# Moving the six hash-bit transfers of each head pair from SyncE's DMA queue to GpSimd's, in a hash attention with a PReLU feed-forward

## The chip, the cores and the metric

The kernel runs on one core of a Trainium2 chip. The metric is the device time of one execution in microseconds (us), as the median of several runs. Five engines work side by side: PE (TensorE) multiplies matrices, DVE (VectorE) and ACT (ScalarE) work on elements, POOL (GpSimd) does odd jobs, and SP (SyncE) only issues DMAs. A DMA can be issued from SP, ACT or POOL. Each engine takes its instructions in order, and an instruction that has to wait holds up everything behind it on the same engine. That is true of SP's queue of DMA issues as well.

## The reference

For 4 batches, 8 heads, 768 positions and 64 dimensions, queries attend only to keys with the same hash bucket of six bits. The result is put through a feed-forward layer with a PReLU.

```python
q_bits = (np.einsum('bhsd,dk->bhsk', q, proj) > 0)       # proj: 64 x 6
k_bits = (np.einsum('bhsd,dk->bhsk', k, proj) > 0)
q_bucket = np.sum(q_bits * 2 ** np.arange(6), axis=-1)   # k_bucket likewise
mask = q_bucket[:, :, :, None] == k_bucket[:, :, None, :]
scores = np.where(mask, np.matmul(q, k^T) / 8, -1e9)
attn = softmax(scores)                                   # sum + 1e-9
x = (attn @ v), heads side by side                       # 3072 x 512
h = x @ w_in                                             # 512 x 2048
out = (np.maximum(h, 0) + alpha * np.minimum(h, 0)) @ w_out
```

## The kernel before

The program computes a guarded fast path, `fast_path`; a second path, `general_path`, would run only if a flag computed on the way said that the inputs are out of the range of the fast one. The profiled execution is the fast path.

It has two stages. In the first, which takes up to about 343 us, it goes through 16 pairs of heads (`pi`), and between them prepares the weights. In the second it runs the two products of the feed-forward layer, on PE nearly without a gap. Most compute instructions are kept in the order in which the program text has them, by a helper called `do`. DMAs are not written through `do` in the place of the change; the scheduler puts each into its queue.

The mask is not applied as such. Each query and each key gets a vector of plus and minus ones from its hash bits, and one extra bf16 matmul adds their product to the scores; where the bits agree the exponent is kept, elsewhere it falls far below. So `scores` needs, for every pair, the hash bits in the layout of its own matmuls: `qb`, one of two buffers of 128 x 768 bf16 whose other rows stay zero, and `kb`, a single buffer of 128 x 1152 bf16. In `kb` the columns are three parts of 384: part 0 and part 1 hold the key bits of the two halves of the positions, and part 2 is where the second half arrives from the Sign.

For pair `pi + 1` this is done while pair `pi` is being attended. In order on PE for one pair:

1. `scores` (L742): 12 cells, a cell being a key block `kc` (0 to 5) and a query half `g` (0 or 1), in the order kc 0 g 0, kc 0 g 1, kc 1 g 0 and so on. In a cell each of two heads has a bf16 matmul of the bits (`sc<-qb,kb`) and an fp32 matmul (`sc<-qT,kT`). ACT takes the exponent (L745).
2. `hash_bits` of the next pair (L704): 16 matmuls in the profile. ACT turns the result into signs (L710) and writes parts 0 and 2 of `kb`. Then six DMAs put the bits into place: four `qb<-kb` of 24 KB (L715) and two `kb<-kb` of 48 KB (L717).
3. `turn` of the pair after that: transposes of q and k (L674).
4. `attend` of this pair (L775): 96 matmuls, about 7.9 us.
5. `totals` (L789): row sums of the exponents, after DVE has added them up (L757, L758, L761, L764).

Then the scores of the next pair follow. The first cell reads query bits of half 0 (the first two DMAs, one for each head), the second cell those of half 1 (the third and the fifth), and the cells from kc 3 on read key bits of half 1 (the fourth and the sixth).

Before the change all six stand in SP's queue, beside these others: the loads of q and k (L499) and v (L488), loads of raw weights (`load_weight`, L566), stores of prepared weights (L634 and L647) and stores of the attention output (L823). In most pairs the built order on SP is three L715, one L566, then L717, L715, L717; in four pairs an L634 stands behind that L566. The weight work that these wait for is on DVE: `weight_clamp` (L590), `weight_parts` (L596), `weight_sum` (L621 and L624).

For the first pair, the bits are written by ACT and DVE directly (L723, L729) and no such DMA is issued. The other 15 pairs use the six DMAs each: 60 of L715 and 30 of L717 in all.

POOL has only some memsets at the start and, in the second stage, 16 DMAs of 512 KB: `load_out` (L962) and `sum_out` (L969).

Of the kernel before, what the change touches and what calls it, by code (L numbers as in the profile page):

```python
# [407 lines left out]
def fast_path(  # L408
# [12 lines left out]
    nc = tc.nc  # L421
    P = 128
    B, H, S, D = q.shape
# [56 lines left out]
    nat, tr, bits = {}, {}, {}  # L480
# [58 lines left out]
    raw, wx, wr = {}, {}, {}  # L539
# [122 lines left out]
    def two_banks(name):  # L662
        return psum.tile([P, 2, 512], F32, name=name, tag="sc", bufs=3)
# [23 lines left out]
    def hash_bits(pi, halves=BOTH, engine=None):  # L687

        if halves.start == 0:
            bits["q", pi] = qbs[pi % 2]
            kb = pool.tile([P, 3 * CW], BF16, name=f"kb{pi}", tag="kb", bufs=1)
            bits["k", pi] = kb[:, :S]
            bits["raw", pi] = kb.rearrange("p (a w) -> p a w", w=CW)
        ps = {"k": two_banks(f"hs{pi}")}
        ps["q"] = psum_av.tile([P, 2, 512], F32, name=f"hsq{pi}", tag="av") if engine is DVE else ps["k"]
        for half in range(halves.start, halves.stop):
            for name in "qk" if engine is DVE else "kq":
                for s in range(2):  # L700
                    r, c = D * s, D * (s ^ half) + 32 * "kq".index(name)

                    for t, c in [("k", c)] + ([("q", c ^ D)] if engine is DVE and name == "q" else []):
                        do(PE.matmul(  # L704
                            ps[t][c : c + 32, half if t == "k" or engine is not DVE else 0, :CW], wh[r : r + D],
                            tr[name, pi][r : r + D, half * CW : (half + 1) * CW], start=True, stop=True,
                        ))
        if engine is None:
            raw = bits["raw", pi]
            do(ACT.activation(raw[:, 0:3:2], ps["k"][:, :, :CW], AF.Sign, bias=hb))  # L710
            for half in range(2):
                for s in range(2):
                    c = D * (s ^ half)
                    cols = slice(half * CW, (half + 1) * CW)
                    nc.sync.dma_start(bits["q", pi][D * s : D * s + 32, cols], raw[c + 32 : c + 64, 2 * half])  # L715
                    if half:
                        nc.sync.dma_start(bits["k", pi][D * s : D * s + D, cols], raw[c : c + D, 2])  # L717
            return
        for half in range(halves.start, halves.stop):
            cols = slice(half * CW, (half + 1) * CW)  # L720
            for s in range(2):
                c = D * (s ^ half ^ (engine is DVE)) + 32
                do(ACT.activation(  # L723
                    bits["q", pi][D * s : D * s + 32, cols], ps["q"][c : c + 32, 0 if engine is DVE else half, :CW], AF.Sign, bias=hb[c : c + 32],
                ))

            for to, c, n in [(0, 0, P)] if half == 0 else [(0, D, D), (D, 0, D)]:
                dst, src = bits["k", pi][to : to + n, cols], ps["k"][c : c + n, half, :CW]
                do(DVE.tensor_scalar(  # L729
                    dst, src, hb_k[c : c + n, 0:1], hb_k[c : c + n, 1:2], op0=ALU.is_gt, op1=ALU.subtract,  # L730
                ))
# [383 lines left out]
    for half in (first, second):  # L1115
        turn(0, "q", half)
        turn(0, "k", half, DVE)
        if half is first:
            nil[0]()
            hash_bits(0, first, DVE)  # L1120
# [10 lines left out]
    ahead = [(kc, 0) for kc in range(CH)]  # L1131
    scores(0, ahead)
    hash_bits(0, second, DVE)
    turn(1, "q")
    turn(1, "k", BOTH, DVE)
# [4 lines left out]
    for pi in range(NPAIR):  # L1140
# [26 lines left out]
        if pi + 1 < NPAIR:  # L1167
            hash_bits(pi + 1)
# [126 lines left out]
```

## Time and profile before

| What | Value |
|---|---|
| time, median of 3 runs | 897.59 us (897.15 to 897.98) |
| time of the profiled execution | 897.64 us |
| its span, first to last instruction | 895.8 us |
| PE busy | 884.2 us, 99% |
| DVE busy | 746.8 us, 83% |
| ACT busy | 379.5 us, 42% |
| POOL busy | 14.4 us, 2% |
| mean granted clock of PE | 0.997 |
| L715, `qb<-kb` on SP | 60, median 585 ns each to issue, 2.4 us to landing |
| L717, `kb<-kb` on SP | 30, median 560 ns each to issue, 3.5 us to landing |

The span is what the profile shows from the first instruction to the last; the time of the same execution is 1.84 us longer. In lines of the timeline and the chain of waits the first number is the start in us from the beginning of the span and the second is the duration in us; `x3` is a number of merged instructions. `SPq` is an issue on SP's queue. In lists of waits the three numbers are the total in us, how often, and the longest. In the views of one source line, a duration is given as the least, the median and the largest, in ns. An issue ends when the issuing engine is done with it; the data lands later, and "to landing" counts from the start of the issue.

### The profile page before, as it was taken

The numbers are of one execution on the slowest core, as the hardware profiler recorded it, in microseconds if no ns is written. First come the engines' busy times: TensorE is split into PE (matmuls) and PEld (weight loads), VectorE is DVE, ScalarE is ACT, GpSimd is POOL, SyncE is SP. The second block draws the span as 40 slices with busy tenths as digits, with TensorE's granted clock in tenths as the row PEclk, the third lists the DMA queues.
The fourth block names the chain that finished last, engine by engine and source line by source line (L and its number), as shares of the span: only waits on it lengthen the run. The fifth ranks groups of instructions, "written<-read, shape, count | busy, mean of one in ns | idle before, by whom it ended". The sixth has DMA issues, their size and how long they took to land.

```text
span 895.8 us, 15331 instructions
## 1 busy us (share of the span) xinstructions
PE 884.2 (99%) x5886; PEld 598.5 (67%) x5886; DVE 746.8 (83%) x1266; ACT 379.5 (42%) x668; POOL 14.4 (2%) x30
## 2 busy tenths in 40 slices
PE   9999999999999999999999999999999999999996
PEld 4544545555555545557997557997557998556996
DVE  5888888888989887899989678988668989768996
ACT  7877777788877762222112222112222111222111
POOL 1000000000000001120000000000000000000000
PEclk9999999999999999999999999999999999999998
DMA  8444575575685625587333435343525242430242
GB/s 235 139 143 129 151 232 153 149 229 173 204 281 163 202 74 185 181 296 289 141 113 107 163 111 166 107 147 88 178 88 192 95 159 80 157 116 0 95 143 72
DMA packets 126177, 137.22 MB, mean 153 GB/s; under 512 B 78976, under 2 KB 110224, under 8 KB 122512
## 3 DMA queue, kind: packets, MB, share of 16 engines
q1 hardware_dynamic: 121376, 126.59, 44.9%
q0 software_dynamic: 2304, 8.39, 2.6%
q10 hardware_dynamic: 2416, 1.18, 0.5%
q8 instruction: 48, 0.79, 0.3%
q14 instruction: 33, 0.27, 0.1%
HBM read 104.87 MB, written 28.31 MB: 149 GB/s over the span
## 4 chain that ended last, share of the span: by engine, by line
PE 84%; DVE 9%; issue 3%; ACT 2%; DMA 2%; SPq 0%; DVEq 0%; ACTq 0%
PE sc L742 12%; PE av L775 10%; PE f_0a L875 2%; PE z_4a L875 2%; PE z_7a L875 2%; PE z_3a L875 2%; PE z_6a L875 2%; PE z_5a L875 2%; PE f_4a L875 2%; PE f_3a L875 2%; PE f_2a L875 2%; PE f_1a L875 2%; PE z_2a L875 2%; PE f_5a L875 2%; DMA qb<-kb 2%
## 5 line engine op out<-in xcount | busy, mean ns | idle before, releaser
L745 ACT ACTIVATE pt<-sc 128x768 f32<-128x768 f32 x192 | 154.8, 812 | 53.5 <-PE sc L742 53.2
L742 PE MATMUL sc<-qT,kT 64*128 64x384 f32 x768 | 155.8, 483 | 0.0
L775 PE MATMUL av<-pt,vn 128*32 128x385 f32 (+1 forms) x1536 | 127.4, 486 | 0.0
L742 PEld LDWEIGHTS sc<-qT,kT 64*128 64x128 f32 x768 | 70.0, 187 | 40.9 <-issue 40.7
L775 PEld LDWEIGHTS av<-pt,vn 128*32 128x32 f32 x1536 | 48.7, 109 | 71.1 <-issue 70.5
L928 DVE TENSOR_TENSOR g<-g,g 128x384 f32<-128x384 f32 x128 | 68.4, 555 | 2.2
L742 PE MATMUL sc<-qb,kb 64*128 64x384 bf16 x384 | 66.5, 323 | 2.4 <-DMA qb<-kb 2.1
L992 DVE TENSOR_TENSOR gs<-g,gs 128x768 f32<-128x768 f32 x56 | 53.3, 952 | 1.0
L992 DVE TENSOR_TENSOR gs<-g 128x768 f32<-128x768 f32 x56 | 53.3, 951 | 0.0
L984 DVE TENSOR_TENSOR ws<-wl 128x512 f32<-128x512 f32 x56 | 38.5, 687 | 17.5 <-DMA wl<-w_out_s 15.9
L753 DVE TENSOR_TENSOR accp<-pt,pt 128x1536 f32<-128x1536 f32 x16 | 28.1, 1759 | 17.5 <-ACT pt L745 17.5
L924 DVE SCALAR_TENSOR_TENSOR g<-h,alpha 128x384 f32<-128x384 f32 x32 | 19.7, 616 | 25.1 <-ACT h L917 25.1
L742 PEld LDWEIGHTS <-kb 64*128 64x128 bf16 x384 | 20.9, 94 | 25.9 <-issue 4.3
L580 ACT ACTIVATE wr<-raw 128x512 int32<-128x512 uint32 x32 | 22.8, 712 | 17.2 <-issue 16.0
L758 DVE TENSOR_TENSOR accd<-accd,pt 128x1536 f32<-128x1536 f32 x16 | 28.1, 1759 | 2.0 <-ACT wr L580 0.5
L761 DVE TENSOR_TENSOR accp<-accp,pt 128x1536 f32<-128x1536 f32 x16 | 28.0, 1753 | 0.0
L757 DVE TENSOR_TENSOR accd<-pt,pt 128x1536 f32<-128x1536 f32 x16 | 28.0, 1752 | 0.0
L764 DVE TENSOR_TENSOR accd<-accd,accp 128x1536 f32<-128x1536 f32 x16 | 28.0, 1751 | 0.0
L805 DVE STREAM_TRANSPOSE st<-sm 128x192 f32<-128x192 f32 x32 | 10.3, 361 | 16.9 <-PE sm L789 16.9
L875 PE MATMUL f_0a<-x,wi 128*128 128x384 f32 x64 | 23.5, 489 | 0.0
L875 PE MATMUL f_4a<-x,wi 128*128 128x384 f32 x64 | 23.3, 486 | 0.0
L875 PE MATMUL f_1a<-x,wi 128*128 128x384 f32 x64 | 23.3, 486 | 0.0
(348 smaller groups left out, 1732.1 us busy)
## 6 DMA issues: line engine op xcount, KB each, us to landing
wi<-w_in_s SPq DMA_DIRECT2D x32, 896.0 KB, 4.7
wl<-w_out_s SPq DMA_DIRECT2D x16, 1024.0 KB, 4.8
wl<-w_out_r SPq DMA_DIRECT2D x12, 1024.0 KB, 4.9
raw<-in_moe_w_out_dram SPq DMA_DIRECT2D x16, 512.0 KB, 3.9
raw<-in_moe_w_in_dram SPq DMA_DIRECT2D x16, 512.0 KB, 4.0
w_in_s<-wsi SPq DMA_DIRECT2D x16, 448.0 KB, 5.8
vn<-in_v_dram SPq DMA_DIRECT2D x16, 384.0 KB, 4.2
x_s<-x SPq DMA_DIRECT2D x16, 384.0 KB, 2.8
```

The source lines that it names most:

```text
L742: do(PE.matmul(sc[:, s, :CW], what["k", pi][r, ks], what["q", pi][r, qs], start=first, stop=not first,))
L745: do(ACT.activation(pts[kc][:, g, :, :CW], sc[:, :, :CW], AF.Exp, scale=SCALE / DOWN))
L753: do(DVE.tensor_tensor(accp[pi], p(0), p(1), op=ALU.add))
L757: do(DVE.tensor_tensor(accd[pi], p(3), p(4), op=ALU.add))
L758: do(DVE.tensor_tensor(accd[pi], accd[pi], p(5), op=ALU.add))
L761: do(DVE.tensor_tensor(accp[pi], accp[pi], p(2), op=ALU.add))
L764: do(DVE.tensor_tensor(accd[pi], accd[pi], accp[pi], op=ALU.add))
L775: do(PE.matmul(av[pi][D * s + t : D * s + t + 32, g, :w], nat["v", pi][:, s, kc * D + t : kc * D + t + 32], pts[kc][:, g, s, :w], start=(k ...
L875: do(PE.matmul(self.ps[bank], self.left(left, k), self.right(right, k), start=start and k == 0, stop=k == self.nk - 1, skip_group_check=no ...
L928: do(DVE.tensor_tensor(new_g(b, to)[:, i], g_m[b, x][:, i], g_m[b, y][:, i], op=ALU.subtract))
L984: do(DVE.tensor_tensor(t, w2[b, n, x], w2[b, n, y], op=op))
L992: do(DVE.tensor_tensor(t, g2[b, n, x], g2[b, n, y], op=ALU.subtract))
```

## The change

In `hash_bits`, the six DMAs of a pair are issued with `nc.gpsimd.dma_start` in place of `nc.sync.dma_start`. What they copy, and what they must wait for, is as before.

```diff
                 for s in range(2):
                     c = D * (s ^ half)
                     cols = slice(half * CW, (half + 1) * CW)
-                    nc.sync.dma_start(bits["q", pi][D * s : D * s + 32, cols], raw[c + 32 : c + 64, 2 * half])
+                    nc.gpsimd.dma_start(bits["q", pi][D * s : D * s + 32, cols], raw[c + 32 : c + 64, 2 * half])
                     if half:
-                        nc.sync.dma_start(bits["k", pi][D * s : D * s + D, cols], raw[c : c + D, 2])
+                        nc.gpsimd.dma_start(bits["k", pi][D * s : D * s + D, cols], raw[c : c + D, 2])
             return
```

## The prediction

> **What bounds the kernel now.** I read the page first, for the engine that never rests and for the chain that ended last.
>
> ```profile
> PE 884.2 (99%) x5886; PEld 598.5 (67%) x5886; DVE 746.8 (83%) x1266; ACT 379.5 (42%) x668; POOL 14.4 (2%) x30
> ...
> PE 84%; DVE 9%; issue 3%; ACT 2%; DMA 2%; SPq 0%; DVEq 0%; ACTq 0%
> ```
>
> PE is busy for 884 of 895.8 us, so only what makes PE wait, or what it stops waiting for, can move the end. POOL does almost nothing. Next, who PE waited for: of all DMAs, only those the change moves.
>
> ```profile
> PE sc L742 <- DMA qb<-kb: 2.1, 4, 1.1
> ```
>
> So four of the 15 pairs that hash their bits through DMA start their scores late. The chain of waits, cut to one of them, shows how:
>
> ```profile
> 89.67 0.70 DVE wso L624
> ...
> 90.39 0.38 SPq L634
> ...
> 90.87 0.51 SPq L717
> ...
> 91.43 4.09 DMA qb<-kb
> ...
> 95.56 0.59 PE sc L742 x2
> ```
>
> SP's queue holds, in this order: three bit copies (numbers 1 to 3), the weight load L566, in the four late pairs also the weight store L634, then copies 4 to 6 (L717, L715, L717). L566 waits for DVE's L621 and L634 for DVE's L624, so copies 4 to 6 stand behind DVE work that has nothing to do with them. SP's own timeline in a pair where PE is not late has the same hole:
>
> ```profile
> 64.53 2.42 SPq L715 DMA_DIRECT2D qb<-kb  x3
> ...
> 69.07 0.33 SPq L566 DMA_DIRECT2D raw<-in_moe_w_in_dram  x1
> 69.50 0.51 SPq L717 DMA_DIRECT2D kb<-kb  x1
> 70.05 0.59 SPq L715 DMA_DIRECT2D qb<-kb  x1
> 71.10 0.50 SPq L717 DMA_DIRECT2D kb<-kb  x1
> ```
>
> The Sign (L710) ends at 64.51. Copy 5 is issued 5.5 us later although its data was there at once; it lands 3.3 us on, at 8.8. PE needs copies 1 and 2 at 73.39 (8.9 us after the Sign, the first cell of scores), 3 and 5 at 74.20 (9.7, the second cell, query half 1), 4 and 6 only at the seventh cell, 4.0 us further (13.7). In the pair at 85.11 the L634 store pushes copy 5 to 91.43 and its landing to 4.1 us: it lands at 95.52, 10.4 after the Sign, past 9.7.
>
> What the lateness costs is seen in the period. The chain has the attend steps at these starts:
>
> ```profile
> 64.91 7.89 PE av L775 x96
> ...
> 106.87 7.89 PE av L775 x96
> ...
> 127.48 7.89 PE av L775 x96
> ```
>
> An undisturbed pair takes 20.61 us (106.87 to 127.48). The two pairs from 64.91 to 106.87 take 41.96, 0.75 more than two undisturbed ones. By the same sums the chain gives 0.66 (127.48 to 169.35) and 0.61 (231.17 to 272.99). In the fourth, PE's timeline has attend at 293.53 and 314.05: 20.52, in a pair without the 1.46 us of transposes, so 1.37 late. **Together 3.4 us.** The 2.1 in the list of waits is less because the rest shows as longer matmuls around the wait.
>
> **What the Trainium skill says.** "DMA: Bandwidth & Descriptors", section "Issuing engines are not separate DMA queues": DMAs from any engine run on the same 16 DMA engines; another issuer saves only sequencer time. The trace agrees that issue order is what hurts here. The same page, "Queues, rings and completion order", has each queue's ring consumed in order and the DMA engines taking turns between rings. That fits copy 5 landing in 4.1 us behind the 512 KB L566 and L634, against a 1.8 us minimum for L715; no run here shows the turns themselves. Its section "Anatomy of one DMA — SWDGE (gpsimd) path" prices a GpSimd DMA at about 2.0 us plus bytes over 436 GB/s. For 512 KB that is an estimate of 3.2; the fastest of L962 took 3.7. "SBUF — State Buffer", section "Who interferes with whom": a VectorE operation in a two-port mode and a GpSimd instruction exclude each other from a shared port pair, and descriptor writing is such an instruction; operations with two SBUF inputs conflict only with GpSimd reads. In the trace DVE's two-input sums keep their length beside POOL's DMAs (L928: 2.21 us for four, at 362.98 beside one and at 353.64 beside none); no one-input case stands beside a POOL DMA.
>
> **The change part by part.** The built program keeps the order of all instructions on PE, DVE and ACT. 60 copies of L715 and 30 of L717 leave SP and stand on POOL between its memsets and L962.
>
> *Removed from SP:* 90 issues at about 0.58 us, some 52 us of queue time. This is worth nothing by itself: no engine waits for SP's other loads in this stage. They go some 2 us earlier in each pair (qn at 69.4 instead of 71.7), and the weight load L566 still waits for DVE. vn is first read by attend two pairs, some 40 us, later.
>
> *Added to POOL:* six issues per pair. The nearest rows are those of the other GpSimd DMAs:
>
> ```profile
> L962 POOL DMA_DIRECT2D wo<-w_out_r x8: 751/756/890, 348.1 to 392.6; - x8
> ...
> DMA to landing us min/median/max: 3.7/6.8/10.8
> ```
>
> and POOL's timeline, in which they follow each other without a gap:
>
> ```profile
> 348.07 3.13 POOL L962 DMA_DIRECT2D wo<-w_out_r  x4 [345.23 <-DVE x L822]
> ```
>
> So 0.78 us per issue, for 512 KB; 24 and 48 KB have fewer rows and should not cost more. POOL has nothing else until L962 at 348, after the last copy (321), so nothing useful queues behind. The waits on POOL are the Sign for copy 1, PE's previous scores for copy 4 (over before the Sign) and semaphores of older copies, some 0.04 us each, 0.2 in all. Starts after the Sign: 0, 0.8, 1.6, 2.5, 3.3, 4.1. From start to landing: below, the page's price, 2.0 + 0.06; above, the fastest 512 KB row, 3.7. Copy 5 lands at 5.4 to 7.0, and I take 6.4. It is needed at 9.7, so 2.7 to 4.3 us are spare. Copy 2 lands at 2.9 to 4.5 against 8.9, copy 6 at 6.2 to 7.8 against 13.7. The cover is the 7.9 us of attend and the row sums on PE.
>
> *Removed from PE:* the four late starts, **-3.4 us**. Eleven pairs with the same engine work show 20.6 us without a wait, so nothing else is late next at that place; the rest of the kernel is PE's and moves up.
>
> *DVE beside POOL's descriptors:* the only one-input SBUF operation on DVE in POOL's 4.9 us is L596, which at 0.42 us for 512 elements runs faster than the 0.69 of L621.
>
> ```profile
> 67.89 0.42 DVE L596 TENSOR_SCALAR wx<-wx 128x512 uint32<-128x512 uint32 x1
> ...
> 69.68 1.75 DVE L764 TENSOR_TENSOR accd<-accd,accp 128x1536 f32<-128x1536 f32 x1
> ```
>
> It starts 3.4 us after the Sign, amid copy 5's issue. If it must wait for one issue, it is up to 0.8 late. L764 ends at 71.43 and the row sums start at 72.62, so 1.2 us are spare. The exception is the last hashed pair, where the waits name L764 once (0.2 us): 0.1 spare there, up to 0.7 lost once. I take 0; bounds 0 and +0.7.
>
> Sum: -3.4, bounds -3.8 (better landings of other loads) and -2.7. Against the profiled execution, 897.64 (span 895.8 and 1.84 outside), that is 894.2; the median of the runs, 897.59, is the same within 0.05.
>
> **Rivals.**
> *Slower: GpSimd's transfers are serial.* If its 2.0 us are paid one after another, copy 5 lands at 5 x 2.06 = 10.3, 0.6 past need, in all 15 pairs: +9.0 - 3.4, 903.2. It decides from a landing at 9.9 (15 x 0.23 = 3.4). Against it: the four L962 issues in 3.13 us. For it: no small GpSimd transfer is in the trace.
> *No change: L596 is held for almost two issues.* At 1.35 us the row sums come 0.16 late in 14 pairs and 1.2 in the last: 3.4, 897.6. A hold of 1.5 would give 899.9. Against it: POOL is done 1.5 us after L596's start, and the port should change hands between two issues.
> *Part of the gain:* in the four late pairs another thing (the L634 store with L566, now issued close to the q and k loads) delays PE by half: 895.9.
> That the transfers do not move is excluded by the built order.
>
> **How the numbers follow.** Full gain 0.70 (893.5 to 895.0); part 0.08; held DVE 0.10; serial transfers 0.12. About 0.2%, 1.8 us, is what a measurement can tell from no change: faster is below 895.8, slower above 899.4. Faster 0.70 + 0.03; within 0.05 + 0.07 + 0.01; slower 0.11 + 0.03. The likeliest is 894.2. The range from 893.4 to 897.6 takes in the full and the partial gain and half of the held DVE, some 0.82.
>
> **What would show it.** Right: PE's wait for the copies gone, attend every 20.6 us in all pairs, POOL busy for some 70 us more at about 0.78 us an issue, copy 5 landing 5 to 7 us after L710, L596 within 1 us of its place. Wrong: PE waiting for qb or kb in most pairs, landings over 9 us, issues over 1.5 us, or a new wait of the row sums for L764.

## The result, and the profile after

| | before | after |
|---|---|---|
| median of 6 runs | 897.79 us (897.15 to 899.33) | 894.12 us (893.48 to 894.80) |
| ratio after / before, 95% interval | | 0.9959 [0.9948, 0.9971] |
| profiled execution, its span | 897.64, 895.8 us | 893.73, 891.9 us |
| first Sign to last Sign (ends of L710 on ACT) | 23.50 to 315.18, 291.68 us | 23.03 to 311.33, 288.30 us |

The change makes the kernel 3.7 us faster (2.6 to 4.7 by the interval); 894.2 was predicted. The profiled executions differ by 3.9 in their spans. Of this, 291.68 - 288.30 = 3.4 lies between the first and the last Sign, where the change works. Another 0.47 lies ahead of the first Sign, where the change moves nothing. It is not a part of the gain: in the repeat of the changed kernel below, the first Sign ends at 23.37, and the stretch between the Signs is 288.28 again. This part goes with the clock. The trace's record of the granted clock begins, with the full clock, at 7.22 us in the profile before and at 6.29 in the one after, and the L704 matmuls at about 6.1 us take 0.85 us before and 0.57 after. Half of the 0.93 between these two times is the 0.47; in seven of the twelve profiles of this case the first Sign ends 19.9 us plus half of that time into the span.

The page of the kernel after, engines and chain by engine:

```profile
PE 882.5 (99%) x5886; PEld 594.7 (67%) x5886; DVE 746.8 (84%) x1266; ACT 379.8 (43%) x668; POOL 59.6 (7%) x120
...
PE 93%; DVE 5%; issue 1%; ACT 1%; ACTq 0%; DVEq 0%
```

DMA and SPq, 2% and 0% of the chain before, no longer stand in it. POOL has 90 instructions more and 59.6 - 14.4 = 45.2 us more busy time. The list of PE's waits (total in us, how often, the longest):

```profile
PE nil L515 <- DVE hb L519: 1.2, 1, 1.2
PE z_2c L875 <- DVE m L1013: 0.5, 1, 0.5
PE sm L789 <- DVE accd L764: 0.2, 1, 0.2
PE sc L742 <- DVE kb L729: 0.2, 1, 0.2
```

The wait for `qb<-kb` is gone and none has come in its place. In the chain of waits no attend step comes late any more; between the second and the third of these stand the scores that were late before:

```profile
64.45 7.89 PE av L775 x96
...
85.06 7.89 PE av L775 x96
...
105.66 7.89 PE av L775 x96
```

Twice 20.6, and so in all pairs with the same work on PE; only the second step (20.8, with one more matmul, L535) and the last two (19.15 and 18.8, with fewer) differ. POOL's timeline in that pair, whose Sign ends at 84.65 (in brackets: how long POOL had been idle, and what ended it):

```profile
84.94 1.48 POOL L715 DMA_DIRECT2D qb<-kb  x3 [17.49 <-ACT kb L710]
86.53 0.52 POOL L717 DMA_DIRECT2D kb<-kb  x1
87.05 0.50 POOL L715 DMA_DIRECT2D qb<-kb  x1
87.54 0.52 POOL L717 DMA_DIRECT2D kb<-kb  x1
```

And SP's timeline after the same Sign:

```profile
89.24 0.33 SPq L566 DMA_DIRECT2D raw<-in_moe_w_out_dram  x1
89.93 0.38 SPq L634 DMA_DIRECT2D w_out_r<-wso  x1
90.40 2.04 SPq L499 DMA_DIRECT2D qn<-in_q_dram  x2
```

All six copies are issued by 88.06, 3.4 us after the Sign, and so ahead of L566 and L634, which wait for DVE as before. What one issue costs, and how long after its start the data lands, from the view of line L715:

```profile
L715 POOL DMA_DIRECT2D qb<-kb x60: 496/501/658, 23.7 to 313.7; - x60
...
DMA to landing us min/median/max: 1.6/1.9/4.2
```

Half a microsecond an issue, and 1.9 us in the middle to landing, where SP's copies of the same line needed 2.4. Copy 5 lands 4.0 to 4.4 us after the Sign in nine pairs and 5.2 to 6.0 in six; PE needs it at 9.7.

### The profile page after: what moved, and what is told of

Its sections match the earlier page's. It is cut to its first block, busy times and chain, and to the rows that moved or that the text cites. A ratio compares the mean times of both kernels' runs of the same rounds, so it can differ in the third digit from the quotient of the medians.

```text
span 891.9 us, 15377 instructions
## 1 busy us (share of the span) xinstructions
PE 882.5 (99%) x5886; PEld 594.7 (67%) x5886; DVE 746.8 (84%) x1266; ACT 379.8 (43%) x668; POOL 59.6 (7%) x120
## 4 chain that ended last, share of the span: by engine, by line
PE 93%; DVE 5%; issue 1%; ACT 1%; ACTq 0%; DVEq 0%
PE sc L742 17%; PE av L775 13%; PE f_0a L875 2%; PE z_4a L875 2%; PE z_7a L875 2%; PE z_3a L875 2%; PE z_6a L875 2%; PE z_5a L875 2%; PE f_4a L875 2%; PE f_3a L875 2%; PE f_2a L875 2%; PE f_1a L875 2%; PE z_2a L875 2%; PE f_5a L875 2%; PE z_1a L875 2%; PE f_7a L875 2%
## 5 line engine op out<-in xcount | busy, mean ns | idle before, releaser
L742 PEld LDWEIGHTS sc<-qT,kT 64*128 64x128 f32 x768 | 68.1, 187 | 39.5 <-issue 39.4
L742 PE MATMUL sc<-qb,kb 64*128 64x384 bf16 x384 | 63.3, 323 | 0.3 <-DVE kb L729 0.2
L715 POOL DMA_DIRECT2D qb<-kb x60 | 29.8, 502 | 264.6 <-ACT kb L710 264.6
L742 PEld LDWEIGHTS <-kb 64*128 64x128 bf16 x384 | 19.0, 94 | 27.8 <-issue 4.3
L764 DVE TENSOR_TENSOR accd<-accd,accp 128x1536 f32<-128x1536 f32 x16 | 28.0, 1751 | 0.0
L805 DVE STREAM_TRANSPOSE st<-sm 128x192 f32<-128x192 f32 x32 | 10.3, 361 | 17.2 <-PE sm L789 17.2
```

What stands on the lines that cost most here:

```text
L715: nc.gpsimd.dma_start(bits["q", pi][D * s : D * s + 32, cols], raw[c + 32 : c + 64, 2 * half])
L742: do(PE.matmul(sc[:, s, :CW], what["k", pi][r, ks], what["q", pi][r, qs], start=first, stop=not first,))
```

## The experiments

The question after the result was not whether PE's wait had gone, but why: is it GpSimd's ring, or the place of the copies ahead of other transfers? And is the margin of 4 to 6 us that is now seen a margin that can be used?

### Four ways to take copy 5 out from behind the store

**Only the store moved.** The six copies stay on SP; the weight stores L634, eight in all, go to GpSimd. One of them stood ahead of copies 4 to 6 in each of the four late pairs.

```diff
-                nc.sync.dma_start(w_out_r[:, :, n].rearrange("m p d -> p m d"), wst[HW + n])
+                nc.gpsimd.dma_start(w_out_r[:, :, n].rearrange("m p d -> p m d"), wst[HW + n])   # L634
```

> The kernel before, with only the eight stores L634 issued by GpSimd; all six bit copies stay on SyncE, still behind L566. Theory (copies 4 to 6 are late only where the store stands ahead of them in SP's queue): copy 5 lands 8.8 us after the Sign in all pairs, under the 9.7 at which it is needed, PE's four late starts vanish, -3.4 us, ratio to before 0.9962. Rival (GpSimd's path is what makes the copies arrive earlier, or SP's 52 us of relieved issue time is what counts): the four late pairs stay, ratio 1.000.

Measured: 893.95 us, ratio 0.9956 [0.9942, 0.9970] (before in these runs: 897.75). SP's timeline in the pair whose store is at 89.59 on POOL:

```profile
84.03 1.86 SPq L715 DMA_DIRECT2D qb<-kb  x3
88.58 0.33 SPq L566 DMA_DIRECT2D raw<-in_moe_w_out_dram  x1
89.01 0.50 SPq L717 DMA_DIRECT2D kb<-kb  x1
89.56 0.58 SPq L715 DMA_DIRECT2D qb<-kb  x1
```

L566 still stands ahead of copies 4 to 6, and copy 5 still lands 8.4 to 9.2 us after the Sign in all pairs but the first and the last, but that is before 9.7, and PE does not wait for a copy. So the 3.4 us are the price of L634's place in the queue, and copies that land late but in time cost nothing.

**Only copy 5 moved.**

```diff
-                    nc.sync.dma_start(bits["q", pi][D * s : D * s + 32, cols], raw[c + 32 : c + 64, 2 * half])
+                    (nc.gpsimd if half and s else nc.sync).dma_start(bits["q", pi][D * s : D * s + 32, cols], raw[c + 32 : c + 64, 2 * half])
```

> The kernel before, with only copy 5 of each pair (L715, second half, second head; 15 DMAs) issued by GpSimd. Theory (the second cell's wait for copy 5 is the whole cost; copies 4 and 6 have 13.7 us): -3.4 us, ratio 0.9962, copies 4 and 6 still landing 10 to 11 us after the Sign in the four pairs with the store, without anyone waiting. Rival (copies 4 and 6 matter too, or all six must leave SP): less than half of the gain, ratio over 0.998.

Measured: 894.13 us, ratio 0.9959 [0.9946, 0.9973]. Copies 4 and 6 still land 10.0 to 11.1 us after the Sign in the four pairs, and nobody waits for them: they are read at 13.7. One transfer of the six carries the whole gain.

**All six on SP, ahead of the bulk.** The weight load and the store are written after `hash_bits`, and GpSimd is not used.

```diff
-        load_weight(i + 4)
         ...
         if pi + 1 < NPAIR:
             hash_bits(pi + 1)
+        load_weight(i + 4)
+        while later:                     # the L634 stores, kept in a list
+            nc.sync.dma_start(*later.pop(0))     # L1170
```

> The kernel before, all six copies on SyncE, but the weight load L566 and the store L634 put behind the six in SP's queue; orders on PE, DVE, ACT and POOL unchanged. Theory (it is the place in the queue, not the issuing engine): copy 5 issued about 2.5 to 3 us after the Sign, landing at 5, no wait of PE for the copies, ratio 0.9962, the same as the change within 0.0015. The weight load goes some 0.5 us later at most, since it waits for DVE until 4.5 us after the Sign and the six issues end at about 3.8. Rival (GpSimd's own ring, or freed SP time, is needed): copies land behind other transfers, gain under half.

Measured: 893.39 us, ratio 0.9951 [0.9937, 0.9964]. SP's timeline:

```profile
84.53 1.85 SPq L715 DMA_DIRECT2D qb<-kb  x3
86.48 0.55 SPq L717 DMA_DIRECT2D kb<-kb  x1
87.08 0.59 SPq L715 DMA_DIRECT2D qb<-kb  x1
87.71 0.59 SPq L717 DMA_DIRECT2D kb<-kb  x1
89.06 0.33 SPq L566 DMA_DIRECT2D raw<-in_moe_w_out_dram  x1
89.79 0.38 SPq L1170 DMA_DIRECT2D w_out_r<-wso  x1
```

The hole of the profile before lies behind the copies now. Copy 5 lands 4.3 to 5.8 us after the Sign, where GpSimd had 4.0 to 6.0. The time cannot be told from that of the change.

**The change once more**, in the same runs, as their measure.

> The changed kernel once more, beside the three above on one chip. All theories: 0.9959 as before within its interval, about 894.1 us. The profiled execution before and after also differ by 0.46 us ahead of the first hashed pair (matmuls of 0.85 us against 0.57 at about 6 us): if that is chance, the time from the first to the last L704 step is the same in this profile as in the first one while the start moves.

Measured: 893.90 us, ratio 0.9958 [0.9944, 0.9972]. The four intervals all lie on each other. What issues the copies is not the reason of the gain; that they, or copy 5 alone, no longer stand behind L634 is.

### Only the harmless copies moved

The opposite test: copies 1 to 3, which never were late, on GpSimd, and 4 to 6 left on SP.

```diff
-                    nc.sync.dma_start(bits["q", pi][D * s : D * s + 32, cols], raw[c + 32 : c + 64, 2 * half])
+                    (nc.sync if half and s else nc.gpsimd).dma_start(bits["q", pi][D * s : D * s + 32, cols], raw[c + 32 : c + 64, 2 * half])
```

> The kernel before, with copies 1, 2 and 3 of each pair on GpSimd and copies 4, 5 and 6 left on SyncE. Theory: copies 1 to 3 were never late (they land 1.8 to 5.7 us after the Sign, needed at 8.9 and 9.7), so nothing is gained: ratio 1.000, PE still waits for qb in four pairs. Rival (relieving SP of 26 us of issue, or GpSimd's ring, brings the gain): about half of -3.4, ratio 0.998.

Measured: 894.23 us, ratio 0.9965 [0.9953, 0.9977] (before: 897.49), the full gain. The expectation missed, and SP's timeline says why:

```profile
84.89 0.51 SPq L717 DMA_DIRECT2D kb<-kb  x1
85.46 0.59 SPq L715 DMA_DIRECT2D qb<-kb  x1
86.09 0.59 SPq L717 DMA_DIRECT2D kb<-kb  x1
89.42 0.34 SPq L566 DMA_DIRECT2D raw<-in_moe_w_out_dram  x1
```

With three issues fewer on SP, the scheduler put copies 4 to 6 ahead of L566, not behind it. The kernel that was run was not the one that was meant. So it was built once more, with the store, the weight load and copies 4 to 6 held in the order of the program text:

```diff
-            nc.sync.dma_start(raw[i], piece(i))
+            do(nc.sync.dma_start(raw[i], piece(i)))                # L566; L634 and copies 4 to 6 likewise
```

> Copies 1 to 3 on GpSimd, copies 4 to 6 on SyncE, as in the earlier run of that name, in which the built order had also moved copies 4 to 6 ahead of L566. Here their place behind L566 and L634 is fixed by program order. Theory (only the place of copies 4 to 6 in SP's queue costs): copy 5 is issued about 5.5 us after the Sign, 6.3 in the four pairs with the store, PE waits there as before, ratio 1.000 (0.998 to 1.001). Rival (taking copies 1 to 3 off SP is worth something by itself, as the earlier run seemed to say): ratio 0.9965.

Measured: 899.79 us, ratio 1.0027 [1.0019, 1.0035] (before: 897.23). No gain but a small loss, outside the expected 0.998 to 1.001 on the side away from the rival. SP's timeline in a pair with a store, and PE's waits for the copies:

```profile
89.90 0.38 SPq L634 DMA_DIRECT2D w_out_r<-wso  x1
90.37 0.46 SPq L566 DMA_DIRECT2D raw<-in_moe_w_out_dram  x1
91.01 0.56 SPq L717 DMA_DIRECT2D kb<-kb  x1
91.62 0.59 SPq L715 DMA_DIRECT2D qb<-kb  x1
```

```profile
PE sc L742 <- DMA qb<-kb: 4.0, 3, 2.3
```

Here copies 4 to 6 are behind both bulk transfers, copy 5 is issued 7.0 us after the Sign (84.61) where it was 6.3 before, and PE is late. That holds in three pairs, which lose 0.97, 1.23 and 4.27 us. Together 6.5 against 3.4 before: the loss comes from the pinned order, which puts L634 ahead of L566 and the copies later still. The order was not held everywhere: in four of the 15 pairs the built program has copies 4 to 6 right after the Sign, ahead of both. One of these is among the four that were late before (Sign at 251.75, L634 at 257.10). Its copy 5 is issued 0.6 us after the Sign, and PE does not wait:

```profile
252.34 0.59 SPq L715 DMA_DIRECT2D qb<-kb  x1
```

So within one kernel, with copies 1 to 3 on GpSimd in every pair, PE is late where copy 5 stands behind L634 and L566 and on time where it does not. Moving three copies to GpSimd with the others left behind L634 gains nothing.

In the pair that loses 4.27 us, only 2.6 are lost at the second cell. The rest is lost by the seventh, where the granted clock is 0.50 for 3.4 us (306.6 to 310.0) after PE's wait of 2.3.

### Is the margin real? GpSimd's copies made later

The prediction called 2.7 to 4.3 us spare, and the profile after shows more. To use up some of it, POOL waits for the Sign with a small copy and then writes zeros to a new tile that nobody reads, 0.74 us each, before it issues the six copies; these go through `do`, so that they stay behind.

```diff
+            do(POOL.tensor_copy(idle[0:32, 0:1], raw[0:32, 2, 0:1]))
+            for _ in range(2):                                       # 4 and 10 in the other two
+                do(POOL.memset(idle, 0.0))
```

The lines move by up to 5: the copies are L720 and L722, the scores L747, L596 is L598, L764 is L769.

> The changed kernel, with one small copy that waits for the Sign and two memsets of 0.73 us ahead of the six transfers on GpSimd (the results of this idle work are not used). The six issues then run from about 2.0 to 5.2 us after the Sign, over DVE's L596, which starts at 3.4. Theory: L596 keeps its place or is late by less than 0.5 us, the row sums keep their 1.2 us of spare time, copy 5 lands at about 6 to 7.5 us, no loss: ratio to before 0.9962. Rival (DVE's one-input operation and descriptor writing exclude each other): L596 starts 0.5 to 1.3 us later or lasts longer, L764 ends later by as much, and the row sums begin to wait in the last hashed pair: up to +1 us.

Measured: 897.86 us, ratio 1.0005 [0.9998, 1.0012]. **The gain is gone**, which was not expected. POOL's timeline (Sign end 84.17) and PE's waits:

```profile
84.30 1.49 POOL L713 COPY idle<-kb 32x1 bf16<-32x1 bf16 x1 [14.58 <-ACT kb L712]
85.85 1.53 POOL L715 MEMSET idle<- 128x768 bf16 x2
87.33 1.70 POOL L720 DMA_DIRECT2D qb<-kb  x3
89.02 0.52 POOL L722 DMA_DIRECT2D kb<-kb  x1
89.53 0.50 POOL L720 DMA_DIRECT2D qb<-kb  x1
```

```profile
PE sc L747 <- DMA qb<-kb: 2.6, 4, 0.7
```

Copy 5 starts 5.4 us after the Sign, 3 later than in the changed kernel. With the 1.6 us that it needed there it would land at 7.0. It lands at 9.4 to 10.7 in all pairs but the first and the last, 4.1 to 5.3 us after its start. Six pairs have their second cell late, by 0.22, 1.05, 0.86, 0.07, 0.92 and 1.00, 4.1 together, and the stretch between the first and the last Sign is 292.37 us, 4.1 more than 288.30. The new thing beside the copies is on SP, at 88.74 and behind:

```profile
88.74 0.33 SPq L568 DMA_DIRECT2D raw<-in_moe_w_out_dram  x1
89.43 0.38 SPq L636 DMA_DIRECT2D w_out_r<-wso  x1
89.90 2.10 SPq L501 DMA_DIRECT2D qn<-in_q_dram  x2
```

The same transfers start at the same place after the Sign in the changed kernel, but there the copies have been issued already. How busy the DMA engines are in those microseconds is seen in a pair without a store in the repeat of the change, by windows of 2 us from the Sign on (window; its length; busy time and number for PE, PEld, DVE, ACT, POOL; granted clock; DMA share; GB/s):

```profile
126.20:128.20 2.00, 2.00 (x28) 0.86 (x30) 1.90 (x2) 2.00 (x4) 1.48 (x3) 1.00 0.16 44
128.20:130.20 2.00, 2.00 (x32) 0.84 (x28) 1.97 (x3) 2.00 (x4) 1.66 (x3) 1.00 0.20 54
130.20:132.20 2.00, 2.00 (x32) 0.83 (x28) 1.97 (x3) 0.89 (x4) 0.00 (x0) 1.00 0.41 79
132.20:134.20 2.00, 2.00 (x32) 0.80 (x24) 0.92 (x1) 0.65 (x2) 0.00 (x0) 1.00 0.89 276
```

For 4 us after the Sign the engines are nearly free; from the seventh on they are full. The copies of the change run in the free stretch, those of this kernel in the full one.

> The same with four memsets: the six issues run from about 3.5 to 6.6 us after the Sign. Theory (copy 5 is needed only at 9.7 us; in the changed kernel it lands at 4.0 to 5.7): it lands at 7.4 to 9.1, still in time, no loss: ratio 0.9962. Rival (the software path has less to spare than that, because other loads share the DMA engines at that moment): PE waits in several pairs, +1 us or more.

Measured: 915.20 us, ratio 1.0198 [1.0184, 1.0212]; no loss was expected, and the rival of the expectation came true. The issues run from 4.9 to 7.9 us after the Sign, where SP starts L568 at 5.1, and copy 5 lands at 10.7 to 12.3 in all pairs but the first and the last, 0.9 to 2.6 after 9.7. Copies 1 to 3 land at 7.9 to 11.2 there and are late as well, so that PE waits at several cells of a pair:

```profile
PE sc L747 <- DMA qb<-kb: 10.2, 23, 0.9
```

The stretch between the Signs is 309.94 us, 21.6 more than with the change. The waits are half of that; the rest stands in longer matmuls around them, as 3.4 us were lost in the kernel before where the waits were 2.1, and in one pair the granted clock is 0.50 for 3.4 us.

> The same with ten memsets: the six issues run from about 8.2 to 11.3 us after the Sign. Theory (the serial rival of the prediction, made real): copy 5 lands at 12.2 to 14 us, 2.5 to 4 us too late in each of 15 pairs, which PE loses in full: +37 to +60 us on the changed kernel, 931 to 954 us, ratio 1.037 to 1.062. If lateness were covered elsewhere, the loss would be well under 30 us.

Measured: 1008.78 us, ratio 1.1253 [1.1226, 1.1281], far over the expected 931 to 954. The issues run from 9.7 us after the Sign and not from 8.2, copy 5 lands at 13.6 to 17.4 in all pairs but the last, 4 to 8 late, and PE waits 76.9 us in 24 places. The span is 113 us longer than with the change, so PE loses the lateness in full and more. What is left, 36 us, goes with the clock. In each of the 15 pairs the granted clock is 0.50 for 3.4 to 10.2 us from about the end of the wait on, 82 us in all, and a cell that takes 0.81 us otherwise takes 1.6 then. The windows view has one such stretch, behind waits of 3.72, 0.31 and 0.78 us:

```profile
120.00:122.00 2.00, 2.00 (x10) 1.26 (x8) 0.00 (x0) 0.81 (x1) 0.00 (x0) 0.50 0.00 0
```

Half of 82 is 41 us; this is an upper estimate of the loss, since PE is idle in part of the time. From the second cell to the seventh a pair takes 4.6 to 9.0 us in place of 4.04, later waits included. In the kernel before and in the one with two memsets, where no wait for a copy is longer than 1.1 us, the clock has no such stretch in this stage.

**Which transfer lengthens the landing?** The kernel with two memsets again, and the q and k loads (L501) held behind the v load (L490) in the program's order, so that they come later. The v load goes through `do` too; only one line of the edit is shown.

```diff
-            queue.dma_start(nat[name, pi][:, cs, s], src[b, 2 * hp + s].rearrange("(p c) d -> p c d", c=NC)[:, cs])
+            (do if pi > 2 else (lambda x: x))(queue.dma_start(nat[name, pi][:, cs, s], src[b, 2 * hp + s].rearrange("(p c) d -> p c d", c=NC)[:, cs]))
```

> The kernel with two memsets ahead of the transfers (copy 5 issued at 5.4 us, landed at 9.4 to 10.7), with the q and k loads L499 of the later pairs put behind the v load L488 in SP's queue, so that they start some 8 us after the Sign instead of 5.4. Theory (copy 5 took 4 to 5 us to land there because those loads filled the DMA engines from 5 us on): copy 5 lands at 7.5 to 9, under 9.7, no wait of PE for the copies, ratio 0.9962. If GpSimd's own issue or the weight load L566 alone makes the landing long: copy 5 over 9 us, ratio near 1.000.

Measured: 898.58 us, ratio 1.0016 [1.0009, 1.0023] (before: 897.23), where 0.9962 was expected. Copy 5 lands at 8.8 to 9.2 in the ordinary pairs, some 0.6 earlier than in the kernel with two memsets alone (9.4 to 9.9), and still at 10.3 to 11.1 in the pairs with a store. So the q and k loads are the smaller part. The pairs of the two kernels have different company for copy 5 when it is issued 5.4 us after the Sign, and that splits the rest:

| Beside copy 5 | Pairs | Start to landing, us |
|---|---|---|
| nothing of SP's yet (the change, issued at 2.4 to 2.8) | nine | 1.6 to 1.8 |
| the 512 KB store alone | last pair, both kernels | 2.9 and 3.0 |
| the 512 KB load alone | ordinary pairs, late loads | 3.4 to 3.9 |
| the load, then q and k loads | ordinary pairs, two memsets | 4.1 to 4.5 |
| load and store, q and k loads later or none | Sign at 293.11, two memsets; four pairs, late loads | 4.9 to 5.7 |
| load and store, then q and k loads | three pairs, two memsets | 5.1 to 5.3 |

Load and store each lengthen the landing, and together they make most of it. The time is not better because a late q load, and behind it a late k load (0.6), now hold PE:

```profile
PE tp_q L676 <- DMA qn<-in_q_dram: 1.2, 1, 1.2
```

### DVE beside GpSimd

In the changed kernel the last issue ends 3.4 us after the Sign, just as L596 begins, so the prediction's doubt about L596 was not put to the test by the change. The kernel with two memsets does so: its issues last from 87.33 to 90.55, and DVE's timeline has

```profile
87.53 0.42 DVE L598 TENSOR_SCALAR wx<-wx 128x512 uint32<-128x512 uint32 x1
```

L596's usual 0.42 us, in the time of the first issue. That one took 0.72 us instead of 0.50, and the three 1.70 instead of 1.48: POOL's side gave way, by 0.2. So it is in all 15 pairs. With four memsets it is a memset that runs at that time:

```profile
112.56 3.29 POOL L715 MEMSET idle<- 128x768 bf16 x4
...
114.24 0.93 DVE L598 TENSOR_SCALAR wx<-wx 128x512 uint32<-128x512 uint32 x1
```

0.93 in place of 0.42, in all 15 pairs, and the memsets took 3.29 for four times 0.74 = 2.95. The sums end 0.5 us later (7.4 after the Sign, before 6.9), which costs PE only in the last hashed pair, as the prediction had placed it:

```profile
PE sm L794 <- DVE accd L769: 0.7, 1, 0.7
```

## Why the prediction was right, and what in it was wrong

*The bound and the mechanism: right.* Ahead of the second stage PE was held by copy 5 alone, in four pairs, through L634's place in SP's queue. Taking the store away, or copy 5, or changing the order on SP, each gives what the change gives; moving only copies 1 to 3, with the order held, gives nothing.

*The size: right.* Minus 3.4 was read from the attend periods, and the stretch between the Signs is 3.4 shorter. The list of PE's waits (2.1) would have been too small. One count was loose: nine pairs before have the period of 20.6 us, not eleven; the other two without a wait have other work.

*Added to POOL: right in sign, three terms mis-sized, the two larger ones to the safe side.* The 512 KB rows gave 0.78 us an issue and 3.1 to landing of copy 5; the small copies took 0.50 and 0.52, and 1.6. The start was put at 0 and is 0.3 us after the Sign, which goes the other way. Together, copy 5 lands at 4.0 to 6.0 and not at 6.4. The busy time grew by 45 us and not by 70. The price of the Trainium skill, "DMA: Bandwidth & Descriptors", section "Anatomy of one DMA — SWDGE (gpsimd) path" (about 2.0 us plus the bytes), was nearer than the nearest row in the profile, and even it is above the fastest, 1.6. A row of another size is a poor price where its bytes make most of it.

*"2.7 to 4.3 us are spare": wrong as a statement on the margin.* The step took the landing time as a property of the copy. The runs show it to go with the moment. Copy 5 needs 1.6 us while the DMA engines are nearly idle and 4.1 to 5.3 once L566, L634 and the q loads run, so 3 us of delay were enough to lose everything. The prediction had quoted both kinds from the profile before, 1.8 us at the least and 4.1 behind L566 and L634, and did not carry them into the margin. The step did not hurt the number because the changed kernel issues early. As far as the working goes that is luck: it did not ask when those transfers start. Even the free stretch is not all alike. In five pairs of the change copy 5 needs 3.0 to 3.4 us. In these the trace has a 16 KB transfer of queue q8 (instruction) that starts 3.2 to 3.5 us after the Sign, as in no other pair; in the first of them L566 starts then too. No run took that transfer away, so its part is not shown.

*The reading of rings: right where it expected no shield, left unsaid where it mattered.* The prediction quoted, from the same page, section "Issuing engines are not separate DMA queues", that another issuer does not bring other DMA engines. The delayed runs agree: with the late loads, copy 5 on GpSimd's ring, issued at 5.4 us beside the load alone, lands 3.4 to 3.9 later; on SP in the kernel before, issued at 5.5 behind the same load, it took 3.1 to 3.6 in the ordinary pairs. But section "Queues, rings and completion order" was used for the engines' taking turns, and the working did not draw from it that a late copy on its own ring would be slowed too.

*Held DVE: the cover was another than the one named.* It was argued that L596 would lie amid copy 5's issue and lose less than 1.2 us. It did not lie there. "SBUF — State Buffer", section "Who interferes with whom", has a two-port VectorE operation and a GpSimd instruction exclude each other. The trace fits that for the memset (0.42 becomes 0.93). For descriptor writing, DVE lost nothing and POOL 0.2 us.

*The rivals.* Serial transfers are refuted: six copies are issued in 3.1 us and all have landed by 4.7 in eight pairs, by 7.2 in all. A partial gain is refuted by the attend period, 20.6 in the four pairs with the store as elsewhere (the last of them 1.37 shorter than before). That SP's relief would be worth nothing holds as far as the profile tells: L566 and L634 still wait for DVE, and no DMA is in the chain.

What stays open: whether the 16 KB transfers of q8 cause the longer landings beside them, and what share of the 36 us in the kernel with ten memsets is the clock.

## What to carry to other kernels

When a small, urgent transfer lands late, read the issuing queue's timeline for what stands ahead of it and what that waits for: here a change of order on the same queue is worth as much as another engine. After an edit to a queue, read the built order again, since a scheduler may move what was not touched, as with copies 4 to 6. And do not carry a landing time to another moment: a margin of 5 us that rests on idle DMA engines was gone here after 3.

## What the runs showed of the hardware that was not expected

- GpSimd issues a copy of 24 or 48 KB within SBUF in 0.50 or 0.52 us and a DMA of 512 KB in 0.75; on SP it is the other way round, 0.59 and 0.56 for the copies and 0.33 for the 512 KB load.
- GpSimd's 24 KB copies land 1.6 us after the start of their issue at the earliest and in a median of 1.9 in the changed kernel; beside 512 KB transfers of another queue copy 5 took 3.4 to 5.3.
- A late transfer can cost more than PE's wait for it: in the kernel with ten memsets each pair's wait of 3.1 us or more came with a granted clock of 0.50 for 3.4 to 10.2 us.
- A POOL copy of 32 x 1 elements, which reads SBUF, ends 0.04 us after DVE's two-input sum L762 in all 15 pairs of the kernel with two memsets. It took 0.475 us where it began shortly before that end, and 1.4 to 1.5 elsewhere. In the pair shown it ended at 85.79:

```profile
84.00 1.75 DVE L762 TENSOR_TENSOR accd<-pt,pt 128x1536 f32<-128x1536 f32 x1
```

  This fits the section "Who interferes with whom" named above, by which an operation with two SBUF inputs conflicts with GpSimd's reads. It is why two memsets of 0.74 us delayed the copies by 3 us and not by 1.5.
